# Moving a first-stage store from SyncE's DMA queue to ScalarE's, one butterfly into the next chunk

## The chip, the core and the metric

The kernel runs on one core of a Trainium2 chip. The metric is device microseconds of one execution, the median over runs. Within the core, PE (TensorE) does matmuls, DVE (VectorE), ACT (ScalarE) and POOL (GpSimd) do elementwise work, and SP (SyncE) only issues DMA transfers here. ACT can issue them too, in line with its own instructions. In the trace the transfers that SP issues are queue q1, and those of ACT queue q10; both are carried by the core's 16 DMA engines.

## The reference

```python
u = x * v                                   # x, v: [2, 12480, 128]
h = (np.maximum(pos_emb @ w1, 0) @ w2) * window   # the filter, [12480, 128]
y = np.fft.irfft(np.fft.rfft(u, n=2 * S, axis=1) * np.fft.rfft(h, n=2 * S, axis=0), n=2 * S, axis=1)[:, :S]
x = (x * y).reshape(24960, 128)
h = x @ w_in                                # [24960, 2048]
return np.maximum(0.01 * h, h) @ w_out      # [24960, 128]
```

A long convolution of two batches with one filter (through a Fourier transform), a product with x, and a two-layer MLP over all tokens, all in float32.

## The kernel before

The transform is split in two stages of sizes 98 and 128. **The first stage of batch 0**, the part that this change touches, transforms batch 0 and the filter together. It runs over 16 chunks `c` of `MC` = 4 columns. For a chunk,

- `load_a(c)` brings in the transform matrices `ft` and the tiles `xt` and `vt` (seven DMAs, three of them large: 300.1 KB, 384 KB and 384 KB; the others carry the few rows that don't fit the pattern). `load_pos` brings in the positions `pos` for four chunks at once (three DMAs, 768 KB the large one).
- `prep(c)` makes the operands two chunks ahead: on POOL the product `uh` = x·v and `q1`, on DVE `q2`, on both the second matrix `f1` from `q1` and `q2`, on PE `pt` and `hp` with ACT's copy `pts` between them, and on DVE the filter part of `uh`. It is a generator of which one piece follows each butterfly.
- four **butterflies** `mm` follow: eight matmuls into `a` (line 314), ACT's copy `a1s` (line 98), and DVE's sum and difference into the tile `o` (lines 100 and 102).
- `store` writes `o` to the scratch `scr1` in DRAM, two DMAs of 588 KB each (line 287).

The program is written out by hand (`manual_schedule`): on each engine the instructions stand in the order in which the code gives them, and each waits for what it needs. SP gives out loads and stores in one line: at the head of chunk `c` come `load_a(c + 3)`, the positions when due, in chunk 2 also six loads of constants (`mb`, `mi`, `mi2`), and only then the store of chunk `c - 1`, which was put off in the list `late`. The tile `o` has two buffers, so DVE can't begin chunk `c + 1` before the store of chunk `c - 1` has landed. `ft` has five, `xt` and `vt` three each. Every DMA raises one of eight counters (DMAHW0 to DMAHW7 in the rows below), which are dealt out in turn over both queues, and it waits until the DMA that had the same counter before it has landed; so at most eight are under way.

Behind the 16 chunks follow the second stage of batch 0 (it reads `scr1` into `bin`), and the first stage of batch 1 and the MLP, which are interleaved.

Of the kernel before, what the change touches and what calls it, by code (L numbers as in the profile page):

```python
# [20 lines left out]
MC = 4  # L21
# [6 lines left out]
def tile_conv_mlp(ctx, tc, x, v, pos_emb, w1, w2, w_in, w_out, cf, cr, cg, cb, ci, cw, out):  # L28
    nc = tc.nc
# [14 lines left out]
    scr1 = dram.tile([128, NA, 2 * C0], F32, name="scr1")  # L44
# [18 lines left out]
    def load_tokens(t, src, m0, n):  # L63

        full = src[: ROWS * NB, :].rearrange("(a p n) d -> a p n d", p=2, n=HB)
        for r in (slice(0, R0), slice(R0, ROWS)):
            nc.sync.dma_start(out=t[r], in_=full[r, :, m0:m0 + n, :])
        last = src[ROWS * NB + m0:ROWS * NB + m0 + n, :]
        nc.sync.dma_start(out=t[ROWS:], in_=last[None, None, :, :].to_broadcast([1, 2, n, last.shape[1]]))
# [24 lines left out]
    def add_sub(pool, a0, a1, dst0, dst1, view, bufs):  # L94

        a1s = pool.tile([128, 512], F32, tag="a1s", name="a1s", bufs=bufs)[:a1.shape[0]]
        n = a1.shape[1]
        nc.scalar.copy(a1s[:, :n], a1)  # L98
        yield
        nc.vector.tensor_tensor(out=dst0, in0=view(a0), in1=view(a1s[:, :n]), op=ALU.add)  # L100
        yield
        nc.vector.tensor_tensor(out=dst1, in0=view(a0), in1=view(a1s[:, :n]), op=ALU.subtract)

    def run(g):
        for _ in g:
            pass


    def chunk(c):
        k0 = c * KC  # L110
        return k0, min(KC, NA - k0)
# [46 lines left out]
    with tc.manual_schedule():  # L158
# [3 lines left out]
        def fetch_a(c):  # L162
            ft = s0.tile([128, MC1 * 4 * NA], F32, tag="s0", name="ft1", bufs=3)[:NA].rearrange(
                "a (m p e) -> a m p e", m=MC1, p=2)
            nc.sync.dma_start(out=ft, in_=cf[:, c * MC1:(c + 1) * MC1])
            xv = []
            for i, src in enumerate((x, v)):
                t = s0.tile([128, 1024], F32, tag=f"s{1 + i}", name="xv1", bufs=3 - i)[:NA, :2 * MC1 * D].rearrange(
                    "a (p m d) -> a p m d", p=2, d=D)
                load_tokens(t, src[1], c * MC1, MC1)  # L170
                xv.append(t)
            got[c] = ft, xv
# [3 lines left out]
        def mult_a(c):  # L176
            ft, (xt, vt) = got.pop(c)
            nc.gpsimd.tensor_tensor(out=xt, in0=xt, in1=vt, op=ALU.mult)
            u1[c] = ft, xt

        with ExitStack() as st:
# [5 lines left out]
            PQ = 16  # L187
# [3 lines left out]
            def load_pos(q):  # L191
                pos_t[q] = sba.tile([NA, 2, PQ, FO], F32, tag="pos", name="pos")
                load_tokens(pos_t[q], pos_emb, q * PQ, PQ)

            def load_a(c):
                ft = sba.tile([NA, MC, 2 * NA], F32, tag="ft", name="ft", bufs=5)
                nc.sync.dma_start(out=ft, in_=cf[:, c * MC:(c + 1) * MC, 0])
                xt = sba.tile([NA, 2, MC, D], F32, tag="xt", name="xt", bufs=3)
                vt = sba.tile([NA, 2, MC, D], F32, tag="vt", name="vt", bufs=3)
                load_tokens(xt, x[0], c * MC, MC)  # L200
                load_tokens(vt, v[0], c * MC, MC)
                f_t[c], xv_t[c] = ft, (xt, vt)
                if c < 2:
                    f1_t[c] = sba.tile([NA, MC, 2 * NA], F32, tag="f1", name="f1", bufs=3)
                    nc.sync.dma_start(out=f1_t[c], in_=cf[:, c * MC:(c + 1) * MC, 1])
# [41 lines left out]
            NC0 = HB // MC  # L247
# [12 lines left out]
            run(prep(1))  # L260
            late = []
            for c in range(NC0):
                if c + 3 < NC0:
                    load_a(c + 3)
                    if (c + 3) * MC % PQ == 0:
                        load_pos((c + 3) * MC // PQ)
                if c == 2:
                    nc.sync.dma_start(out=mb, in_=cb)
                    nc.sync.dma_start(out=mi, in_=ci)
                    for s in range(2):  # L270
                        for ri in range(2):
                            nc.sync.dma_start(out=mi2[HB * s:HB * s + HB, ri], in_=ci[HB * ri:HB * ri + HB, s])
                if c == 6:
                    for m, mh, ml in ((mb.rearrange("p s r q -> p s (r q)"), mb_h, mb_l), (mi, mi_h, mi_l)):
                        nc.scalar.copy(mh, m)
                        nc.vector.tensor_tensor(out=ml, in0=m, in1=mh, op=ALU.subtract)
                for f in late:
                    f()
                late = []
                uh, ft, f1 = uh_t.pop(c), f_t.pop(c), f1_t.pop(c)  # L280
                nxt = prep(c + 2) if c + 2 < NC0 else iter(())
                o = sba.tile([NA, 2, MC, 2, C0], F32, tag="o", name="o")

                def store(m0, n, o, c=c):
                    for ri in range(2):
                        r0 = HB * ri + c * MC + m0
                        nc.sync.dma_start(out=scr1[r0:r0 + n].rearrange("m k e -> k m e"),
                                          in_=o[:, ri, m0:m0 + n].rearrange("a m s d -> a m (s d)"))
                if c == 7:
                    w22 = s0.tile([128, D], F32, tag="mi", name="w22", bufs=1)  # L290
                    for i in range(2):
                        nc.sync.dma_start(out=w22[64 * i:64 * i + 64, :], in_=w2)
                if c == NC0 - 3:
                    fetch_a(0)

                    bin0 = s0.tile([128, MC1 * 4 * NA], F32, tag="s0", name="bin0", bufs=3)[
                        :, :KC * 2 * C0].rearrange("p (k s e) -> p k s e", k=KC, s=2)

                def early():
                    for ri in range(2):  # L300
                        rows = slice(HB * ri, HB * ri + HB - DIR * MC)
                        nc.sync.dma_start(out=bin0[rows], in_=scr1[rows, :KC, :].rearrange("p k (s e) -> p k s e", s=2))

                def direct(m, o, c=c):
                    for ri in range(2):
                        r0 = HB * ri + c * MC + m
                        nc.sync.dma_start(out=bin0[r0:r0 + 1], in_=o[:KC, ri, m])
                if c == NC0 - 1:
                    mult_a(0)
                for mm in range(MC):  # L310
                    a = psa.tile([NA, 2, 512], F32, tag="a", name="a", bufs=3)
                    for p, f, n in ((0, ft, NA), (1, f1, ROWS)):
                        for ri in range(2):
                            nc.tensor.matmul(a[:, p, C0 * ri:C0 * ri + C0], f[:n, mm, NA * ri:NA * ri + NA],  # L314
                                             uh[:n, p, mm], start=True, stop=True)
                    run(add_sub(sba, a[:, 0, :2 * C0], a[:, 1, :2 * C0], o[:, :, mm, 0, :], o[:, :, mm, 1, :],
                                lambda t: t.rearrange("a (r e) -> a r e", r=2), 2))
                    next(nxt, None)
                    if c >= NC0 - DIR:
                        direct(mm, o)  # L320
                    if c == NC0 - 1 and mm == EARLY:
                        early()
                    if c == NC0 - 1 and mm == MC - 1:
                        store(0, MC, o)
                if c < NC0 - 1:
                    late.append(lambda store=store, o=o: store(0, MC, o))
# [161 lines left out]
        with ExitStack() as st:  # L488
# [70 lines left out]
            late = []  # L559
# [40 lines left out]
            for c in range(NCH):  # L600
# [10 lines left out]
                late = []  # L611
                n = chunk(c)[1]
# [234 lines left out]
```

## Time and profile before

| | |
|---|---|
| median of 3 runs | 1793.81 us (1793.01 to 1794.57) |
| the profiled execution | 1797.53 us, of which its span is 1795.5 us |
| mean granted TensorE clock | 0.979 |
| PE busy over the span | 1714.1 us (95%) |
| DVE, ACT, POOL busy | 966.5, 892.5, 587.2 us (54%, 50%, 33%) |
| bytes moved by the DMA engines | 251.77 MB |

The table is of the whole span, most of which is the MLP, where PE is nearly always at work. The first stage of batch 0 takes about the first 167 us and is read by itself, in the rows below: times there are microseconds from the start of the span.

### The profile page before, as it was taken

The numbers are of one execution on the slowest core, as the hardware profiler recorded it, in microseconds if no ns is written. First come the engines' busy times: TensorE is split into PE (matmuls) and PEld (weight loads), VectorE is DVE, ScalarE is ACT, GpSimd is POOL, SyncE is SP. The second block draws the span as 40 slices with busy tenths as digits, with TensorE's granted clock in tenths as the row PEclk, the third lists the DMA queues.
The fourth block names the chain that finished last, engine by engine and source line by source line (L and its number), as shares of the span: only waits on it lengthen the run. The fifth ranks groups of instructions, "written<-read, shape, count | busy, mean of one in ns | idle before, by whom it ended". The sixth has DMA issues, their size and how long they took to land.

```text
span 1795.5 us, 29288 instructions
## 1 busy us (share of the span) xinstructions
PE 1714.1 (95%) x10620; PEld 1607.7 (90%) x10620; DVE 966.5 (54%) x1688; ACT 892.5 (50%) x1803; POOL 587.2 (33%) x450
## 2 busy tenths in 40 slices
PE   6787989879999999999999999999999999999998
PEld 6677545479999999999999999999999999999998
DVE  3566788845455555555555544444444444444444
ACT  1222444324445666666666666444444444444444
POOL 3453334213323555555544444211121111211120
PEclk8789999989999999999999999999999999999999
DMA  9898999786756465555555541212211122112210
GB/s 224 244 274 259 310 301 321 235 248 192 216 159 180 121 179 142 140 144 144 144 144 144 141 129 54 77 50 65 60 50 50 54 64 57 51 50 60 65 51 14
DMA packets 147707, 251.77 MB, mean 140 GB/s; under 512 B 10842, under 2 KB 96742, under 8 KB 144492
## 3 DMA queue, kind: packets, MB, share of 16 engines
q1 hardware_dynamic: 127420, 224.21, 44.8%
q10 hardware_dynamic: 20144, 25.69, 4.3%
q8 instruction: 84, 1.38, 0.3%
q14 instruction: 59, 0.48, 0.1%
HBM read 166.37 MB, written 83.43 MB: 139 GB/s over the span
## 4 chain that ended last, share of the span: by engine, by line
PE 84%; DMA 9%; DVE 3%; SPq 2%; issue 1%; ACT 1%; POOL 0%; ACTq 0%; POOLq 0%; DVEq 0%
PE mh L693 10%; PE mh L695 10%; PE mh L694 10%; PE acc L713 10%; PE acc L712 10%; PE acc L714 10%; PE yp L679 6%; PE cv L132 4%; PE cv L350 2%; DMA scr<-o 2%; PE up L117 2%; PE dp L139 2%; DMA xt<-in_x_dram 2%; PE op L723 2%; DMA ft<-in_cf_dram 1%; PE xp L671 1%
## 5 line engine op out<-in xcount | busy, mean ns | idle before, releaser
L699 DVE SCALAR_TENSOR_TENSOR rl<-mh,rh 128x390 fp32r<-128x390 f32 x1024 | 574.9, 564 | 616.6 <-ACT rh L698 614.9
L698 ACT ACTIVATE rh<-mh 128x390 fp32r<-128x390 f32 x1024 | 508.1, 498 | 387.3 <-PE mh L695 369.9
L693 PE MATMUL mh<-zh,w_in_h 128*128 128x390 f32 x1024 | 366.0, 357 | 0.0
L695 PE MATMUL mh<-zh,w_in_l 128*128 128x390 f32 x1024 | 350.2, 342 | 0.0
L694 PE MATMUL mh<-zl,w_in_h 128*128 128x390 f32 x1024 | 349.4, 341 | 0.0
L713 PE MATMUL acc<-rl,w_out_h 128*128 128x390 f32 x1024 | 348.8, 341 | 0.0
L712 PE MATMUL acc<-rh,w_out_h 128*128 128x390 f32 x1024 | 348.3, 340 | 0.0
L714 PE MATMUL acc<-rh,w_out_l 128*128 128x390 f32 x1024 | 348.2, 340 | 0.0
L686 POOL TENSOR_TENSOR zl<-zf,zh 128x390 fp32r<-128x390 f32 x63 | 64.9, 1030 | 706.1 <-ACT zh L685 706.1
L693 PEld LDWEIGHTS mh<-zh,w_in_h 128*128 128x128 f32 x1024 | 194.0, 189 | 2.2 <-DVE rl L699 0.2
L694 PEld LDWEIGHTS mh<-zl,w_in_h 128*128 128x128 f32 x1024 | 193.9, 189 | 2.2 <-DVE zl L686 0.2
L695 PEld LDWEIGHTS mh<-zh,w_in_l 128*128 128x128 f32 x1024 | 194.0, 189 | 0.0
L713 PEld LDWEIGHTS acc<-rl,w_out_h 128*128 128x128 f32 x1024 | 193.9, 189 | 0.0
L714 PEld LDWEIGHTS acc<-rh,w_out_l 128*128 128x128 f32 x1024 | 193.1, 189 | 0.0
L712 PEld LDWEIGHTS acc<-rh,w_out_h 128*128 128x128 f32 x1024 | 193.0, 188 | 0.0
L679 PEld LDWEIGHTS yp<-g,cp 98*128 98x128 f32 x1024 | 123.5, 192 | 0.0
L679 PE MATMUL yp<-g,cp 98*128 98x97 f32 (+1 forms) x1024 | 123.1, 274 | 0.0
L431 POOL TENSOR_TENSOR us<-us,hd 128x512 f32<-128x512 f32 (+1 forms) x50 | 63.6, 1272 | 146.2 <-ACT us L429 146.2
L685 ACT CAST zh<-zf 128x390 fp32r<-128x390 f32 x64 | 33.2, 519 | 148.8 <-DVE zf L684 148.8
L485 POOL TENSOR_TENSOR cp<-cin 98x512 f32<-98x512 f32 x63 | 88.4, 1402 | 0.0
L484 POOL TENSOR_TENSOR cp<-cin 98x512 f32<-98x512 f32 x63 | 81.5, 1293 | 17.5 <-DMA cin<-scr 9.4
L98 ACT COPY a1s<-a 98x384 f32<-98x384 f32 x64 | 30.6, 479 | 110.3 <-PE a L314 67.2
(129 smaller groups left out, 2149.9 us busy)
## 6 DMA issues: line engine op xcount, KB each, us to landing
cin<-scr SPq DMA_DIRECT2D x63, 392.0 KB
hd<-hspec SPq DMA_DIRECT2D x48, 512.0 KB
g<-in_cg_dram SPq DMA_DIRECT2D x64, 300.1 KB
scr<-o SPq DMA_DIRECT2D x32, 588.0 KB
bin<-scr SPq DMA_DIRECT2D x23, 768.0 KB
scr1b<-o SPq DMA_DIRECT2D x32, 392.0 KB
hspec<-hs ACTq DMA_DIRECT2D x48, 256.0 KB
scr<-ct ACTq DMA_DIRECT2D x24, 512.0 KB
```

Of the source, the lines that this page charges most:

```text
L132: nc.tensor.matmul(dst, u, w, start=(i == 0), stop=(i == 2))
L484: eng.tensor_tensor(out=o1, in0=c0, in1=c1, op=ALU.subtract)
L485: eng.tensor_tensor(out=o0, in0=c0, in1=c1, op=ALU.add)
L679: nc.tensor.matmul(yp[:, at:at + n], ci_t[:, r, m, p, :], g[:, r, p, m, :n], start=(r == 0), stop=(r == 1))
L693: nc.tensor.matmul(hp, w_in_h[:, fs], zh, start=True, stop=False)
L694: nc.tensor.matmul(hp, w_in_h[:, fs], zl, start=False, stop=False)
L695: nc.tensor.matmul(hp, w_in_l[:, fs], zh, start=False, stop=True)
L698: nc.scalar.activation(out=rh, in_=hp, func=AF.Relu)
L699: nc.vector.scalar_tensor_tensor(out=rl, in0=hp, scalar=0.0, in1=rh, op0=ALU.max, op1=ALU.subtract)
L712: nc.tensor.matmul(ap, w_out_h[:, f, :], rh, start=False, stop=False)
L713: nc.tensor.matmul(ap, w_out_h[:, f, :], rl, start=False, stop=False)
L714: nc.tensor.matmul(ap, w_out_l[:, f, :], rh, start=False, stop=(f == NF - 1))
```

## The change

The store goes from SP's queue to ACT's. It is given out inside the butterfly loop, behind the first butterfly (`mm` = 0) of the next chunk and ahead of that chunk's piece of `prep`; and the loads of chunk `c + 3`, with the positions, follow it there, where they stood at the chunk's head. The loads of constants in chunk 2 keep their place in the code, which is now ahead of that chunk's loads.

```diff
             for c in range(NC0):
-                if c + 3 < NC0:
-                    load_a(c + 3)
-                    if (c + 3) * MC % PQ == 0:
-                        load_pos((c + 3) * MC // PQ)
                 if c == 2:
...
-                for f in late:
-                    f()
-                late = []
...
-                        nc.sync.dma_start(out=scr1[r0:r0 + n].rearrange("m k e -> k m e"),
+                        nc.scalar.dma_start(out=scr1[r0:r0 + n].rearrange("m k e -> k m e"),
                                           in_=o[:, ri, m0:m0 + n].rearrange("a m s d -> a m (s d)"))
...
+                    if mm == 0:
+                        for f in late:
+                            f()
+                        late = []
+                        if c + 3 < NC0:
+                            load_a(c + 3)
+                            if (c + 3) * MC % PQ == 0:
+                                load_pos((c + 3) * MC // PQ)
                     next(nxt, None)
```

On ACT the difference begins in chunk 0: the first row of three copies is butterflies 2 and 3 of chunk 0 and butterfly 0 of chunk 1; `scr_60` is `scr1`, so that the rows with it are the stores of chunks 0 and 1 (minus: before, plus: after, with what each instruction waits for).

```order
 L98 COPY a1s<-a 98x384 [waits DVE_49,PE_49,Activation_49] x3
+L280 DMA scr_60<-o 98x4x384 [waits DMAHW3_49,DVE_49]
+L280 DMA scr_60<-o 98x4x384 [waits DMAHW5_49]
 L232 COPY pts<-pt 128x392 [waits PE_49]
-L98 COPY a1s<-a 98x384 [waits DVE_49,PE_49,Activation_49] x4
+L98 COPY a1s<-a 98x384 [waits PE_49,Activation_49]
+L98 COPY a1s<-a 98x384 [waits DVE_49,PE_49,Activation_49] x3
+L280 DMA scr_60<-o 98x4x384 [waits DMAHW5_49,DVE_49]
+L280 DMA scr_60<-o 98x4x384 [waits DMAHW0_49]
```

Two store instructions now stand on ACT between the copy of a chunk's first butterfly and its `pts`, and wait there for DVE's last difference of the chunk before (DVE_49) and for a counter each.

On SP, before, from the loads of chunk 5 on (they are given out in chunk 2), with the constants, the store of chunk 1 and the loads of chunk 6 behind them:

```order
L197 DMA ft<-in_cf_dram 98x4x196 [waits DMAHW1_49,PE_49]
L67 DMA xt<-in_x_dram 96x2x512 [waits DMAHW2_49,Pool_49]
L67 DMA xt<-in_x_dram 1x2x512 [waits DMAHW3_49]
L69 DMA xt<-in_x_dram 1x2x512 [waits DMAHW4_49]
L67 DMA vt<-in_v_dram 96x2x512 [waits DMAHW5_49]
L67 DMA vt<-in_v_dram 1x2x512 [waits DMAHW6_49]
L69 DMA vt<-in_v_dram 1x2x512 [waits DMAHW7_49]
L268 DMA mb<-in_cb_dram 128x256 [waits DMAHW0_49]
L269 DMA mi<-in_ci_dram 128x256 [waits DMAHW1_49]
L272 DMA mi_75<-in_ci_dram 64x128 [waits DMAHW2_49]
```

The same place after the change:

```order
L264 DMA mb<-in_cb_dram 128x256 [waits DMAHW3_49]
L265 DMA mi<-in_ci_dram 128x256 [waits DMAHW4_49]
L268 DMA mi_75<-in_ci_dram 64x128 [waits DMAHW5_49]
L268 DMA mi_75<-in_ci_dram 64x128 [waits DMAHW6_49]
L268 DMA mi_75<-in_ci_dram 64x128 [waits DMAHW7_49]
L268 DMA mi_75<-in_ci_dram 64x128 [waits DMAHW0_49]
L197 DMA ft<-in_cf_dram 98x4x196 [waits DMAHW1_49,PE_49]
L67 DMA xt<-in_x_dram 96x2x512 [waits DMAHW2_49,Pool_49]
L67 DMA xt<-in_x_dram 1x2x512 [waits DMAHW3_49]
L69 DMA xt<-in_x_dram 1x2x512 [waits DMAHW4_49]
L67 DMA vt<-in_v_dram 96x2x512 [waits DMAHW5_49]
L67 DMA vt<-in_v_dram 1x2x512 [waits DMAHW6_49]
```

The stores are gone from SP, and the constants stand ahead of the loads of chunk 5. The counters that the two `mi_75` rows with DMAHW5 and DMAHW0 wait for are those that the two stores of chunk 1 raise on ACT.

## Rows read from the trace of the kernel before

**Rows 1.** Busy time of each engine in stretches of the first stage: up to the start of chunk 3 on DVE, chunk 3, chunks 4 to 12, and chunks 13 to 15. The last columns are the granted clock, the mean busy share of the DMA engines and GB/s.

```profile
core 0: us, PE busy (x) PEld busy (x) DVE busy (x) ACT busy (x) POOL busy (x), PEclk, DMA share, GB/s
33.50:56.90 23.40, 17.52 (x109) 16.51 (x108) 13.03 (x23) 5.08 (x11) 12.33 (x8) 0.86 0.83 223
56.90:65.30 8.40, 7.22 (x31) 6.71 (x32) 5.82 (x12) 1.83 (x5) 4.29 (x3) 0.61 0.97 286
65.30:147.80 82.50, 69.55 (x412) 63.76 (x410) 53.10 (x102) 21.99 (x48) 44.93 (x28) 0.88 0.96 273
147.80:167.20 19.40, 15.57 (x82) 14.35 (x82) 13.60 (x27) 4.78 (x10) 3.61 (x3) 0.88 0.80 247
```

**Rows 2.** Who waited for whom on DVE from 35 to 168 us: total, times, longest.

```profile
DVE o L100 <- DMA scr<-o: 43.7, 12, 8.1
DVE o L100 <- ACT a1s L98: 4.4, 5, 1.7
```

**Rows 3.** DVE in order of time: start, duration, line. The last difference of chunk 1, the first sum of chunk 2, the last difference of chunk 2, then the first sum of chunks 3, 4, 6, 7, 13 and 15.

```profile
40.45 0.55 DVE L102 TENSOR_TENSOR o<-a,a1s 98x384 f32<-98x384 f32 x1
43.00 0.56 DVE L100 TENSOR_TENSOR o<-a,a1s 98x384 f32<-98x384 f32 x1 [2.01 <-DMA scr<-o]
48.27 0.54 DVE L102 TENSOR_TENSOR o<-a,a1s 98x384 f32<-98x384 f32 x1
56.91 0.56 DVE L100 TENSOR_TENSOR o<-a,a1s 98x384 f32<-98x384 f32 x1 [8.10 <-DMA scr<-o]
65.29 0.56 DVE L100 TENSOR_TENSOR o<-a,a1s 98x384 f32<-98x384 f32 x1 [2.57 <-DMA scr<-o]
86.60 0.56 DVE L100 TENSOR_TENSOR o<-a,a1s 98x384 f32<-98x384 f32 x1 [6.46 <-DMA scr<-o]
95.23 0.56 DVE L100 TENSOR_TENSOR o<-a,a1s 98x384 f32<-98x384 f32 x1 [2.82 <-DMA scr<-o]
147.79 0.56 DVE L100 TENSOR_TENSOR o<-a,a1s 98x384 f32<-98x384 f32 x1 [2.59 <-DMA scr<-o]
161.58 0.56 DVE L100 TENSOR_TENSOR o<-a,a1s 98x384 f32<-98x384 f32 x1 [3.39 <-DMA scr<-o]
```

**Rows 4.** The chain of work that ended last, where it runs over PE at its full clock in chunk 3 and 4 (16 matmuls are two butterflies), over the last store, and over the store of chunk 1: start, length.

```profile
50.19 6.60 DMA scr<-o
63.49 0.41 PE pt L229 x4
63.91 1.30 PE a L314 x8
65.21 0.88 PE hp L240 x8
169.25 5.64 DMA scr<-o
175.04 4.36 DMA bin<-scr
```

**Rows 5.** SP's queue in order of time: start, time to give out, line. The constants, the store of chunk 1 and the loads of chunk 6, then the positions and the store of chunk 4.

```profile
42.94 0.38 SPq L268 DMA_DIRECT2D mb<-in_cb_dram  x1
45.89 0.36 SPq L269 DMA_DIRECT2D mi<-in_ci_dram  x1
47.09 2.44 SPq L272 DMA_DIRECT2D mi<-in_ci_dram  x4
49.63 1.01 SPq L287 DMA_DIRECT2D scr<-o  x2
50.74 1.07 SPq L197 DMA_DIRECT2D ft<-in_cf_dram  x1
...
74.03 2.48 SPq L67 DMA_DIRECT2D pos<-in_pos_emb_dram  x2
77.42 0.57 SPq L69 DMA_DIRECT2D pos<-in_pos_emb_dram  x1
78.09 0.92 SPq L287 DMA_DIRECT2D scr<-o  x2
```

**Rows 6.** What the DMA engines moved in chunks 4 to 12 (65.3 to 147.8 us): the total, then by queue: packets, MB, share of 16 engines.

```profile
DMA packets 15259, 22.55 MB, mean 273 GB/s; under 512 B 799, under 2 KB 11411, under 8 KB 15252
q1 hardware_dynamic: 15252, 22.46, 95.8%
```

**Rows 7.** The same of a stretch of the second stage (274 to 282 us), in which SP's queue loads `xv` by the same pattern as `xt` and `vt` and ACT's queue stores.

```profile
DMA packets 1659, 3.14 MB, mean 392 GB/s; under 512 B 138, under 2 KB 650, under 8 KB 1658
q1 hardware_dynamic: 585, 1.60, 53.0%
q10 hardware_dynamic: 1073, 1.53, 52.0%
```

**Rows 8.** Columns as in rows 1, two short stretches of the first stage: one of loads of `vt` alone, one of stores alone.

```profile
104.00:106.00 2.00, 1.59 (x10) 1.30 (x9) 2.00 (x5) 0.58 (x2) 0.88 (x1) 1.00 0.99 235
158.00:160.00 2.00, 2.00 (x15) 2.00 (x14) 0.18 (x1) 0.91 (x2) 1.82 (x1) 1.00 0.91 330
```

**Rows 9.** DMA instructions by line: time to give one out, least, median and most, in ns. ACT's stores of the second stage, ACT's `hspec` stores there, and SP's stores of the first stage.

```profile
L148 ACTq DMA_DIRECT2D scr<-ct x22: 364/366/398, 191.1 to 337.3; - x22
L628 ACTq DMA_DIRECT2D hspec<-hs x50: 515/534/1242, 175.7 to 348.4; - x50
L287 SPq DMA_DIRECT2D scr<-o x32: 308/358/1010, 34.9 to 169.3; - x32
```

**Rows 10.** POOL's part of `prep` (chunks 4 to 12): count, busy, mean ns, idle time ahead of it and its releasers. Below it ACT's copy of the first butterfly of chunk 2, and PE's wait for the positions.

```profile
L212 POOL TENSOR_TENSOR uh<-xt,vt 98x1024 f32<-98x1024 f32 x9 | 21.7, 2410 | 19.2 <-DMA vt<-in_v_dram 8.2 <-DMA ft<-in_cf_dram 3.8 <-PE a L314 3.4
L221 POOL TENSOR_TENSOR q<-ft,rot 98x784 f32<-98x784 f32 x10 | 17.2, 1719 | 0.0
40.54 0.48 ACT L98 COPY a1s<-a 98x384 f32<-98x384 f32 x1 [0.82 <-PE a L314]
82.91 0.89 PE L229 MATMUL pt<-ident,pos 98*128 98x98 f32 x4 [3.71 <-DMA pos<-in_pos_emb_dram]
```

## The prediction

> **What bounds the kernel now.** I read the stretches of the first stage first, then DVE's waits, DVE's order of time, SP's queue, and last the DMA queues. In chunks 4 to 12 the DMA engines are busy 0.96 of the time, while DVE works 53.1 of 82.5 us, ACT 22.0 and PE 69.6, a part of that at half clock (granted 0.88 in the mean) [rows 1]. So the stage runs at the pace of its transfers. The place where that is felt is DVE: it waits 12 times, 43.7 us in all, for a store to land before it may write `o` again, and only 4.4 us for ACT [rows 2].
>
> Without waits a chunk takes less than the 9.17 us it has on average between the starts of chunks 4 and 13 ((147.79 - 65.29)/9) [rows 3]. On PE it is four butterflies of 1.30 us, `pt` with 0.41 and `hp` with 0.88, together 6.5 us at full clock [rows 4]; on DVE 53.1/9 = 5.9 us [rows 1].
>
> Two things make a store late. SP gives it out late: the pair of chunk 1 is ready at 41.0 us (DVE's last difference ends at 40.45 + 0.55) [rows 3] and goes out at 49.63, behind the loads of chunk 5 and six loads of constants; the pair of chunk 4 goes out at 78.09, behind the positions [rows 5]. Then it stands in one queue behind those loads. The DMA engines themselves do 2.51 MB per chunk (22.55/9) at 273 GB/s [rows 6].
>
> **The change part by part.** *Issue on ACT.* 30 of the 32 store instructions move into ACT's line ahead of `pts` and the next copy; the last pair moves to ACT too, at the end. ACT gives out a transfer in 0.37 us at the shortest form and about 0.53 at the `hspec` form (SP needs 0.36 for these stores) [rows 9], so about 0.9 us per chunk with the gap between two. ACT works 22.0/82.5 of the time, 2.4 us per chunk [rows 1]; DVE meanwhile has a butterfly (two of about 0.5 us) and `q2`. I cost it at nothing; if that cover were gone it would be 0.9 us for each of 15 chunks, 13.5 us. No store stood in ACT's line in this stage before, so that is the bound of this term.
>
> *The rate of the transfers.* Before, every transfer of this stage is in q1. Loads of `vt` alone run at 235 GB/s and stores alone at 330, both with the engines nearly full (0.99 and 0.91) [rows 8]. With loads of that same pattern in q1 and stores in q10 at once, the second stage moves 392 GB/s, halves of it in either queue [rows 7]. These are the bounds of the new rate: 273, as now, and 392, which would do a chunk's 2.51 MB in 6.4 us. The store rows and the loads here have other row lengths than there, so I take neither end, but about 320, 7.9 us per chunk; that is nearer to the old row, because the loads also have to wait for free counters.
>
> Here a rule of the Trainium skill stands against the change. "DMA: Bandwidth & Descriptors", section "Issuing engines are not separate DMA queues", says that transfers of ACT, SP and POOL run on the same 16 engines, and that giving them out on several "will only save the time on the sequencer it takes to initiate the DMA". By it the rate would stay at 273 GB/s, which is rival 1 below. The 392 GB/s of rows 7 speak against it, without settling it, as the transfers there are not the same.
>
> *How soon a store lands.* Free of SP it goes out 0.3 us after DVE's last difference. Alone it needs 7.2 us from there (given out at 49.63, chunk 3 starts on it at 56.91 [rows 3, 5]; its transfer is 6.60 us on the chain [rows 4], the last store's 5.64). With loads beside it longer; I take 9. As `o` has two buffers, two chunks take 0.3 + 9 + one chunk's own 6.5 us: 15.8, or 7.9 us per chunk, which happens to be the 320 GB/s above. With 7.2 it is 7.0.
>
> *Chunks 2 and 3.* The constants now stand ahead of the loads of chunk 5, and two of them wait for counters that the stores of chunk 1 raise. ACT can send that pair when the copy of butterfly 0 of chunk 2 is done (41.0 us) [rows 10] and the store of chunk 0 has landed, which let DVE start at 43.0 [rows 3]; say 43, landed at 43 + 7.2 = 50.2. DVE could begin chunk 3 there instead of at 56.9. But the fourth `mi` load and the loads of chunk 5 go out only then; they take about 4 us to give out and 2 to land: 56.2. POOL's product and `q1` follow (2.41 + 1.72 [rows 10]): 60.3, and DVE, which waits for `q1` in the middle of chunk 3, still has about 3 us to do: chunk 4 starts at 63.4 instead of 65.3, a gain of 1.9 us. If the store of chunk 0 lands 1.6 us earlier on its own queue, which the shorter line ahead of it allows, it is 3.5. I take 3. So most of the 8.1 us of rows 3 is given back to the late loads.
>
> *Chunks 4 to 12.* Nine chunks of 7.9 instead of 9.17 us: 9 x 1.27 = 11.4 us less. From this goes the wait for the positions: in chunk 6 PE waits for them until 82.9 us [rows 10]. They now wait for a counter of the store of chunk 4, go out some 5 us earlier than at 74.03 [rows 5], and the chunk still stops for them; the stop costs PE its clock as it does now (0.61 in the stretch behind the long wait of chunk 3 [rows 1]). I charge 4.5 us. Left: 6.9 us.
>
> *Chunks 13 to 15 and the end.* There 7.9 us per chunk would be no better than the 19.4 us of now for three [rows 1]; the 3.39 us wait ahead of chunk 15 [rows 3] may go, and the last store, whose landing after 5.64 us releases the second stage [rows 4], stays last. I put 0, with 0 to 3 us of gain.
>
> Sum: 3 + 6.9 + 0 = 9.9 us, about 10. Nothing behind it depends on absolute time: the second stage and the MLP begin when the last store has landed and move forward as a whole. Against the profiled execution, 1797.5 us, this gives 1787.5; that execution stands 3.7 us above the median of the runs, so against the median 1793.8 it is **1784 us**.
>
> **The rivals.** *1. The transfers stay at their rate.* Then only the stretches can gain in which the engines are not full: 0.83 until chunk 3 and 0.80 from chunk 13 on, against 0.96 between [rows 1]. That is 23.4 x 0.13/0.96 = 3.2 us and 19.4 x 0.16/0.96 = 3.2; the first goes back to the late loads of chunk 5. About 3 us remain: 1791. For it speak the 0.96 and the skill's rule; against it rows 7.
>
> *2. Slower: the loads now wait for the stores.* The counters are shared, and after the change a load often has to wait for a store of the chunk just finished, with POOL's 4.1 us still to come after it. If a store beside loads lands later than 11.5 us after it was given out, two chunks take 0.3 + 11.5 + 6.5 = 18.3 us, as now; that is the point from which it decides. At 13.5 us a chunk takes 10.2, and nine of them 9 us more, to which the 3 us of chunks 2 and 3 are no longer gained: about 1802. For it speaks that POOL already waits 8.2 us for `vt` in this stretch [rows 10]; against it that a store needs only 7.2 alone.
>
> *3. The full rate.* At 392 GB/s the transfers need 6.4 us per chunk, and with stores that land in 7.2 a chunk takes 7.0: 9 x 2.2 = 19.5 us, and with 3 + 2 for the ends about 22 us: 1772.
>
> **How the numbers follow.** Runs of this kernel lie within 0.1% of their median; 0.2%, 3.6 us, is about what can be told from no change. Chances: the forecast (1777 to 1789) 0.58, rival 1 0.18, rival 2 0.14, rival 3 0.10. The forecast and rival 3 are faster by more than 0.2%; of rival 1 a fifth is, the rest is within 0.2%, and so is a little of rival 2. Faster 0.71, same 0.17, slower 0.12. The range that leaves out 2 in 10 goes from 1773 (into rival 3) to 1797 (past rival 1, into the nearer part of rival 2); the forecast's own is 1777 to 1789.
>
> **What would show it.** Right: the stores under ACT's queue, with q10 carrying near half of the bytes of chunks 4 to 12; over 300 GB/s there; DVE's waits for stores well under 43.7 us; a new wait in chunk 3 of DVE's second matrix for POOL's `q1`, which started late; chunk 4 near 63, chunk 13 near 138, the start of the second stage's `bin` loads near 165. Wrong: a rate near 273 GB/s (rival 1); waits of ACT's copies or of POOL's product for loads that add up to more than DVE's store waits lose (rival 2). If ACT is held by a full queue when it gives out the second of a pair, the 0.9 us per chunk becomes several, and that alone could turn the sign.

## The result, and the profile after

The changed kernel takes 1805.8 us (median; 1803.0 to 1808.9) against 1794.2 (1793.0 to 1796.7) of the kernel before: 1.0063 times as long, 95% interval 1.0044 to 1.0083. It is slower by 11.6 us, where 1784 was forecast. The profiled execution took 1805.71 us, its span is 1803.6 (1795.5 before).

The same stretches as in [rows 1], cut at the same chunk starts on DVE (chunks 1 to 2, chunk 3, chunks 4 to 12, and from chunk 13 to the last store; columns as there):

```profile
32.90:56.06 23.16, 17.88 (x88) 16.55 (x88) 14.24 (x23) 4.81 (x10) 8.94 (x6) 0.75 0.74 215
56.06:65.24 9.18, 7.93 (x51) 7.11 (x49) 5.88 (x11) 2.31 (x5) 5.34 (x3) 1.00 0.86 266
65.24:154.58 89.34, 68.88 (x396) 64.21 (x396) 59.43 (x101) 21.56 (x47) 51.17 (x27) 0.89 0.86 258
154.58:173.90 19.32, 16.73 (x104) 15.30 (x104) 15.91 (x27) 5.67 (x12) 8.45 (x4) 1.00 0.75 241
```

Chunk 4 starts where it started before (65.24 against 65.29). Chunks 4 to 12 take 89.34 us instead of 82.5, and the DMA engines are busy 0.86 of that instead of 0.96. That is 6.8 of the 8.1 us by which the span grew; the rest falls behind chunk 13.

Who waited for whom from 35 to 174 us, on DVE (against [rows 2]), POOL, PE, and on SP's queue:

```profile
DVE o L100 <- ACT a1s L98: 25.2, 13, 5.7
DVE f L236 <- POOL q L221: 14.7, 8, 3.8
DVE o L100 <- DMA scr<-o: 4.8, 4, 1.7
...
POOL uh L212 <- DMA vt<-in_v_dram: 23.4, 5, 10.7
...
PE pt L229 <- DMA pos<-in_pos_emb_dram: 13.5, 3, 5.2
PE hp L240 <- ACT pts L232: 11.1, 9, 3.1
...
SPq L67 <- DMA scr<-o: 17.8, 6, 6.2
SPq L268 <- DMA scr<-o: 6.3, 1, 6.3
SPq L197 <- DMA scr<-o: 5.2, 2, 3.6
SPq L69 <- DMA scr<-o: 2.2, 2, 1.9
```

DVE's wait for stores has all but gone, as forecast: 4.8 us instead of 43.7. In its place DVE waits 25.2 us for ACT's copies and 14.7 for POOL's `q1`, POOL waits for `vt` (23.4), and SP's queue stands 31.5 us (the last four rows) with a load in hand until a store has landed. Such a load needs a counter that a store of ACT's queue still holds.

DVE also works longer: 59.43 us in chunks 4 to 12 instead of 53.10. Most of that is `q2`, the product that DVE makes for the second matrix (from 35 to 170 us, before and after):

```profile
L221 DVE TENSOR_TENSOR q<-ft,rot 98x784 f32<-98x784 f32 x13 | 14.0, 1075 | 0.0
L221 DVE TENSOR_TENSOR q<-ft,rot 98x784 f32<-98x784 f32 x13 | 22.9, 1763 | 0.0
```

In both traces `q2` takes 0.97 us where POOL is idle as it starts. Where POOL's product or `q1` is already at work, `q2` ends 0.8 to 0.9 us after POOL does (in the changed kernel one `q2` runs from 100.92 to 103.11, and POOL's `q1` ends at 102.28). POOL's work, now later, lengthens `q2` 8 times in 13 instead of twice.

Stations of the chain of work that ended last, and SP's queue around chunk 4 (start, length or time to give out):

```profile
41.72 6.63 DMA scr<-o
48.37 0.53 SPq L268
...
65.65 10.39 DMA scr<-o
76.11 0.61 SPq L67
...
83.63 6.06 DMA pos<-in_pos_emb_dram
89.83 0.89 PE pt L229 x4
```

```profile
72.62 0.35 SPq L197 DMA_DIRECT2D ft<-in_cf_dram  x1
76.11 1.27 SPq L67 DMA_DIRECT2D xt<-in_x_dram  x2
...
82.36 1.23 SPq L67 DMA_DIRECT2D pos<-in_pos_emb_dram  x2
```

Store, load, store, load: the store of chunk 3 takes 10.39 us, the `xt` loads go out only then, 3.1 us after the transfer ahead of them had been given out, the positions behind them, and PE gets its positions at 89.83, 6.9 us later than in [rows 10].

What the engines moved in chunks 4 to 12 (against [rows 6]):

```profile
DMA packets 15541, 23.05 MB, mean 258 GB/s; under 512 B 819, under 2 KB 11516, under 8 KB 15534
## 3 DMA queue, kind: packets, MB, share of 16 engines
q1 hardware_dynamic: 8226, 12.13, 47.3%
q10 hardware_dynamic: 7308, 10.84, 38.3%
```

Near half of the bytes are in q10, as forecast, but the rate has fallen from 273 to 258 GB/s. For a full engine it is 258/0.86 = 300, against 273/0.96 = 284.

### The profile page after: what moved, and what is told of

Read it like the earlier page. It is cut to its first block, busy times and chain, and to the rows that moved or that the text cites. A ratio compares the mean times of both kernels' runs of the same rounds, so it can differ in the third digit from the quotient of the medians.

```text
span 1803.6 us, 29292 instructions
## 1 busy us (share of the span) xinstructions
PE 1717.2 (95%) x10620; PEld 1611.5 (89%) x10620; DVE 981.1 (54%) x1688; ACT 893.6 (50%) x1803; POOL 596.7 (33%) x450
## 4 chain that ended last, share of the span: by engine, by line
PE 84%; DMA 7%; DVE 4%; SPq 2%; issue 1%; ACT 1%; POOL 0%; ACTq 0%; POOLq 0%
PE mh L694 10%; PE mh L696 10%; PE mh L695 10%; PE acc L714 10%; PE acc L713 10%; PE acc L715 10%; PE yp L680 6%; PE cv L132 4%; PE cv L351 3%; PE up L117 2%; DMA scr<-o 2%; DMA vt<-in_v_dram 2%; PE op L724 2%; DMA xt<-in_x_dram 2%; PE dp L139 1%; PE xp L672 1%
## 5 line engine op out<-in xcount | busy, mean ns | idle before, releaser
L485 POOL TENSOR_TENSOR cp<-cin 98x512 f32<-98x512 f32 x63 | 81.5, 1293 | 16.7 <-DMA cin<-scr 16.6
L446 POOL TENSOR_TENSOR pl<-p,ph 128x512 fp32r<-128x512 f32 (+1 forms) x50 | 62.8, 1274 | 40.3 <-ACT ph L445 40.1
```

The lines of the kernel that those rows point to most:

```text
L485: eng.tensor_tensor(out=o1, in0=c0, in1=c1, op=ALU.subtract)
```

## The experiments

Ratios are to the kernel before, timed on the same chip; brackets are 95% intervals. In kernels that move the 4-KB transfers, line numbers are one or two higher (L101 is L100 here).

**Parts of the change.** *e1: loads at the head of the chunk again, ahead of the constants.*

```diff
@@ for c in range(NC0):
+                if c + 3 < NC0: load_a(c + 3); ...load_pos
@@ if mm == 0:
-                        if c + 3 < NC0: load_a(c + 3); ...load_pos
```

> Edit: the changed kernel with the loads of the chunk three ahead given out at the head of the chunk again, ahead of the constants; the stores stay on ACT behind butterfly 0. Theory (loads are held on SP's queue by the completion counters of the stores, which SP's and ACT's transfers share): the loads of chunks 6 and later keep the counters that they have in the changed kernel, so the long holds in chunks 4 to 12 stay; only the constants no longer stand ahead of the loads of chunk 5. About 1803 us, between 1799 and 1806. Rival A (ACT loses the time: the stores stand ahead of its copies): as the changed kernel, 1806. Rival C (giving the loads out a butterfly later is what costs): back to 1794 or faster.

Measured: 1810.7 us, 1.0079 [1.0055, 1.0103], above the range given and within the noise of the changed kernel. With the stores off SP's queue, where the loads stand in the program hardly matters. Chunk 4 now starts at 63.49 on DVE, 1.8 us sooner, and chunk 13 again at 154.6: a lead won early is lost in the middle.

*e2: order alone.*

```diff
-                        nc.scalar.dma_start(out=scr1[r0:r0 + n]...
+                        nc.sync.dma_start(out=scr1[r0:r0 + n]...
```

> Edit: the changed kernel with the stores on SP's queue; the order in the program is that of the changed kernel (store behind the next butterfly 0, loads behind the store). Theory (counters): the last load of chunk c+4 has to wait for the first store of chunk c, as in the changed kernel, one chunk earlier than before the change; the DMA engines starve, and one queue has no faster mix: 1803 to 1812 us, DMA share of chunks 4 to 12 below 0.92. Rival A (ACT's line is what costs): no store stands in ACT's line, so 1790 to 1796. Rival B (the mix of two queues is slower than one): 1794 or faster.

Measured: 1820.7 us, 1.0142 [1.0125, 1.0160], slower than any bound given. In one queue the loads stand behind a store that waits for DVE's last difference (27.6 us in all); the engines are busy 0.83 in chunks 4 to 12, at 232 GB/s:

```profile
68.60:168.20 99.60, 70.13 (x394) 66.92 (x393) 57.83 (x102) 21.56 (x47) 47.27 (x27) 0.81 0.83 232
```

*e3: queue alone* (the kernel before, and only this line):

```diff
-                        nc.sync.dma_start(out=scr1[r0:r0 + n]...
+                        nc.scalar.dma_start(out=scr1[r0:r0 + n]...
```

> Edit: the kernel before with its stores on ACT's queue; they stand at the head of the chunk as before, behind the loads in the program. Theory (counters): the loads wait for the same stores' counters as in the changed kernel, so SP's queue is held 20 to 30 us by stores in the stage and the time is that of the changed kernel within 5 us: 1802 to 1811; the difference to it is what ACT loses when it stands behind DVE's last difference at the head of each chunk. Rival A (ACT's line): clearly slower than the changed kernel, 1812 or more, since ACT now waits for the end of DVE's chunk ahead of the first copy. Rival C (the later place of the loads is what costs): 1784 to 1792.

Measured: 1812.9 us, 1.0097 [1.0077, 1.0118]: the queue alone makes it slower, and neither part by itself gains. The time lies just inside what rival A asked for: ACT's copies wait 35.7 us for stores here (35 to 168 us), 0.8 us in the changed kernel. Together the two parts cost less than either alone. A likely reading, which these waits support and no run tried apart, is that the place behind butterfly 0 spares ACT that wait, and the queue of their own spares the loads the wait for the store to go out (e2).

*p1: q1 ahead of the product on POOL* (the changed kernel):

```diff
@@ def prep(c):
-                (nc.gpsimd if c else nc.vector).tensor_tensor(out=uh[:, :, :, FO:], in0=xt, in1=vt, op=ALU.mult)
@@ behind q1, q2
+                (nc.gpsimd if c else nc.vector).tensor_tensor(out=uh[:, :, :, FO:], in0=xt, in1=vt, op=ALU.mult)
```

> Edit: the changed kernel with the product x * v (L212) behind q1 (L221) on POOL; q1 needs only the first-stage matrices and the rotation, the product needs the loads that come last in a chunk. Theory (counters): the loads are as late as in the changed kernel, but DVE's sum f (L236) no longer waits for q1 behind the product (14.7 us in the changed kernel between 33 and 175 us); the product itself is needed only two chunks on. Some 6 to 13 us less than the changed kernel: 1793 to 1800. Rival A (ACT's line): the wait for q1 was only where ACT's lateness showed; within 3 us of the changed kernel.

Measured: 1808.2 us, 1.0075 [1.0053, 1.0096]: no gain, where 6 to 13 us were expected. DVE's wait for `q1` (14.7 us) is gone from the trace, and PE waits for the positions 28.1 us instead of 13.5. The wait moved.

**Loads without the stores' counters.** *g1: stores on POOL,* whose transfers count on counters of their own:

```diff
-                        nc.scalar.dma_start(out=scr1[r0:r0 + n]...
+                        nc.gpsimd.dma_start(out=scr1[r0:r0 + n]...
```

> Edit: the changed kernel with the stores given out by POOL instead of ACT, at the same place in the program. In the program POOL's transfers count on completion counters of their own, so no load waits for a store. Theory (shared counters hold the loads): SP's queue waits 0 us for the landing of a store in the stage (31 us in the changed kernel), the DMA share of chunks 4 to 12 is back at 0.93 or more; if a store on POOL costs no more than one on ACT, 1780 to 1792 us. What POOL needs to give a transfer out is not known: at more than 2 us per store it would become the bound, with 1800 or more, and SP's waits would tell that apart from the rivals. Rival C (loads and stores of the same chunk get in each other's way at the DMA engines, counters or not): the DMA share stays near 0.86 and the time near 1806.

Measured: 1809.9 us, 1.0082 [1.0065, 1.0100]. SP waits for no store any more, and it is no faster: POOL now stands at the store with the product and `q1` behind it, and DVE's `q2` comes behind them 8 times in 13, 3.3 to 5.5 us each (42.6 us in all, against 14.0 before).

```profile
POOL scr L280 <- DVE o L102: 39.0, 14, 3.5
L221 DVE TENSOR_TENSOR q<-ft,rot 98x784 f32<-98x784 f32 x13 | 42.6, 3273 | 0.0
```

*g2: the four 4-KB transfers of a chunk on POOL,* so that five transfers per chunk share the eight counters, *and g3: the same on the kernel before.*

```diff
@@ load_tokens, for xt and vt of batch 0
-            nc.sync.dma_start(out=t[r], in_=full[r, :, m0:m0 + n, :])
+            (nc.sync if r.start == 0 else nc.gpsimd).dma_start(out=t[r], in_=full[r, :, m0:m0 + n, :])
-        nc.sync.dma_start(out=t[ROWS:], in_=last...
+        nc.gpsimd.dma_start(out=t[ROWS:], in_=last...
```

> Edit: the changed kernel with the four 4-KB transfers of a chunk (rows 96 and 97 of xt and vt) given out by POOL; SP gives out three loads per chunk and ACT two stores. With five transfers per chunk on the eight shared counters instead of nine, the first load that waits for a store waits for one three or more chunks back. Theory (shared counters): SP waits under 5 us for stores, chunks 4 to 12 have a DMA share of 0.93 or more, 1780 to 1792 us, unless four transfers per chunk cost POOL more than about 4 us. Rival A (ACT's line) and rival C (contention at the engines): 1800 or more.

> Edit: the same on the kernel before (the four 4-KB transfers of a chunk given out by POOL), as the control for the run with that edit on the changed kernel: it holds what the edit itself costs on POOL and saves on SP. Theory (shared counters): in the kernel before the loads hardly wait for stores' counters (2.6 us), so there is little to gain but SP's own time: 1788 to 1797. The difference of the two is then the gain of the change without the held loads: the changed kernel with the edit 5 to 12 us ahead of this one. Rivals A and C: this one 8 us or more ahead.

Measured: g2 1803.8 us, 1.0050 [1.0032, 1.0067]; g3 1789.6 us, 0.9971 [0.9960, 0.9981]. The edit helps the kernel before; on the changed one its gain is within the noise, against the theory. In g2 SP's queue still stands 19.6 us for stores (31.5 in the changed kernel, under 5 expected). The loads are nearly in time all the same (POOL's wait for `vt` is 5.3 us instead of 23.4), but DVE waits for stores again and PE for `pts`:

```profile
DVE o L101 <- DMA scr<-o: 22.0, 7, 5.9
...
PE hp L241 <- ACT pts L233: 24.3, 11, 6.6
```

So late loads are one cost and not the whole.

*t1: pts ahead of the stores on ACT* (the changed kernel; the three lines `for f in late` stand behind `next(nxt, None)`):

```diff
@@ if mm == 0:
-                        for f in late: f()
-                        late = []
                         if c + 3 < NC0: load_a(c + 3) ...
                     next(nxt, None)
+                    if mm == 0:
+                        for f in late: f()
+                        late = []
```

> Edit: the changed kernel with the copy of pts ahead of the stores in ACT's line instead of behind them. Rival A (ACT's line): PE's wait for pts ahead of hp (11 us on PE, 9 times) goes, and 5 to 11 us with it: 1795 to 1801. Theory (shared counters): that wait lay beside late loads anyway; what changes the time is which counters the loads get, and here the stores of chunks 1 to 4 wait for each other's counters while loads wait for stores only at chunks 4, 6, 8 and 10: chunk 5 starts up to 4 us earlier than in the changed kernel, and the end is within 5 us of it: 1800 to 1808.

Measured: 1812.4 us, 1.0092 [1.0074, 1.0111]. PE's wait for `pts` is gone, and nothing is won: ACT's copies now wait 10.5 us behind the stores, and PE for the positions 22.4 us. Not the gain that ACT's line as the sole cause would give.

**Two costs taken away, and the third buffer.** *h1: g2 and t1 together; h2: g1 and t1 together* (on POOL that puts the store behind the product and `q1`).

> Edit: the changed kernel with the 4-KB transfers on POOL (which alone gave 1803.8 us, with SP's waits for stores down, but with PE waiting 24.3 us for pts, which stands behind the stores on ACT), and the copy of pts put ahead of the stores. Theory K (ACT's line is the second cost: a store waits there for the counter of an earlier store or for DVE's last difference, and pts, hp and the next butterflies stand behind it): PE's wait for hp goes, 1786 to 1794 us, level with the control of the kernel before (1789.6). Theory N (a store that shares the engines with loads that run ahead lands late, 9.4 to 13.4 us, wherever it stands): DVE's waits for stores stay over 20 us and the time is 1798 to 1806.

> Edit: the changed kernel with the stores on POOL, behind the product and q1 of chunk c+2 instead of ahead of them (ahead, POOL waited 41 us for DVE's last difference with that work behind it: 1809.9 us). No counter is shared with the loads and ACT gives out nothing. Theory K (a store in an in-order line costs what stands behind it): POOL's wait at the store falls under 10 us, PE's wait for POOL's f (18.6 us) goes: 1785 to 1796 us. Theory N (contention at the engines): DVE then waits for stores, which land 10 us or more after they are given out, and the time stays at 1800 or more.

Measured: h1 1800.2 us, 1.0026 [1.0016, 1.0037]; h2 1797.7 us, 1.0010 [0.9992, 1.0027], with runs from 1788 to 1803. From g1 to h2, 0.7% goes with what stands behind the store in POOL's line (`q2` falls from 42.6 to 16.7 us with it, in the fastest of the ten runs, which is the one profiled). In h1 the waits for stores are 27.0 us on DVE, and on its chain of waits a store beside loads takes 12 to 13 us:

```profile
65.69 12.53 DMA scr<-o
...
94.15 13.08 DMA scr<-o
```

In the kernel before, the stores on that chain take 5.40 to 7.55 us (two of them in [rows 4]), with the younger loads behind them in the same queue.

*o3: three buffers of `o`,* on the changed kernel and on the one before.

```diff
-                o = sba.tile([NA, 2, MC, 2, C0], F32, tag="o", name="o")
+                o = sba.tile([NA, 2, MC, 2, C0], F32, tag="o", name="o", bufs=3)
@@ load_a: xt and vt
-                ... bufs=3)
+                ... bufs=2)
```

> Edit: the changed kernel with three buffers of o instead of two (xt and vt get two instead of three for the room). Held loads (the counters) as the cause: DVE waits only 4.8 us for stores in the changed kernel, so there is nothing for a third buffer to give; the loads keep their counters: 1800 to 1808 us. Theory N (late landing of the stores sets the pace of chunks 4 to 12): the landing has a chunk more to hide in, 1790 us or faster.

> Edit: the same on the kernel before, as the control: DVE's 43.7 us of waits for stores should nearly go. If those waits were what the kernel lost (as the prediction took it), 1775 to 1785 us. If the transfers were full anyway (DMA share 0.96 in chunks 4 to 12), the wait turns up at POOL's product or PE's positions and only the stretches with free engines give something: 1788 to 1795.

Measured: changed 1808.9 us, 1.0072 [1.0050, 1.0093]; before 1794.4 us, 0.9994 [0.9983, 1.0004]. The second is the run that decides on the forecast. All waits of DVE in it from 35 to 168 us:

```profile
DVE o L100 <- ACT a1s L98: 21.7, 13, 7.7
DVE f L236 <- POOL q L221: 10.5, 8, 5.8
DVE q L221 <- DMA ft<-in_cf_dram: 0.7, 1, 0.7
```

The 43.7 us of waits for stores are gone, with the stores still on SP, and the kernel is as fast as before. What the engines move between the starts of chunks 4 and 13 is the same too, 272 GB/s at 0.95 busy against 273 at 0.96:

```profile
55.80:143.70 87.90, 66.76 (x398) 63.85 (x397) 60.64 (x103) 21.53 (x47) 50.46 (x27) 0.84 0.95 272
```

In place of the waits for stores DVE has those for ACT and `q1` above, and a longer `q2` (25.8 us instead of 14.0). So the waits were where a stage that was full of transfers let its slack be seen. The edit also takes a buffer each from `xt` and `vt`; what that costs by itself was not run, and the unchanged rate is what speaks against a gain hidden by it.

**What is left.** *k1: h1 with xt and vt in two buffers instead of three. k2: k1 and three buffers of `o`. k3: g3 with the o3 edit. k4: h2 with the o3 edit.*

> Edit: the kernel with the 4-KB transfers on POOL and pts ahead of the stores on ACT (1800.2 us), with two buffers of xt and vt instead of three, so that SP's loads can run one chunk less ahead. Theory N (the stores land late, 12 to 13 us on the chain of waits of that kernel, because loads that are not needed yet share the engines with them): DVE's waits for stores fall well below 27.0 us and the time to 1792 to 1798. If running ahead is not what costs: the loads are later and nothing else changes, 1800 to 1808.

> Edit: as the run before it, and three buffers of o. Now no load waits long for a store's counter, PE does not wait for pts, and a store has a chunk more to land in. What is left is the rate at which two queues move the bytes. If the mix is faster by as much as the prediction took (320 against 273 GB/s): 1780 us or faster, 8 us or more ahead of the control with the same edits on one queue. If the mix gives only what the busy share shows (about 307 against 298 GB/s for a full engine in the two kernels without the third buffer): within 4 us of the control.

> Edit: the kernel before with the 4-KB transfers on POOL (1789.6 us), and three buffers of o, two of xt and vt: the control of the run before it, with the stores on SP's queue. The third buffer gave nothing on the kernel before (1794.4), since the transfers filled the engines 0.95 of the time; the same is expected here: 1787 to 1791 us.

> Edit: the kernel with the stores on POOL behind q1 (1797.7 us, 1788 to 1803), and three buffers of o, two of xt and vt. No counter is shared, ACT gives nothing out. Theory N (late landing beside loads that run ahead): DVE's waits for stores (29.6 us) go and the time falls to 1782 to 1792. If the rate is the limit: 1793 to 1800, as with two buffers.

Measured: k1 1797.0 us, 1.0010 [0.9998, 1.0021]; k2 1794.5, 0.9987 [0.9977, 0.9997]; k3 1788.5, 0.9958 [0.9943, 0.9972]; k4 1789.6, 0.9969 [0.9953, 0.9985]. Chunks 4 to 12 of the four, in that order:

```profile
64.30:145.30 81.00, 67.32 (x413) 63.10 (x411) 65.77 (x101) 21.90 (x48) 65.05 (x61) 0.94 0.95 290
```

```profile
61.60:142.60 81.00, 68.58 (x401) 64.81 (x401) 72.06 (x102) 21.13 (x47) 66.52 (x62) 0.88 0.94 290
```

```profile
58.40:137.20 78.80, 65.17 (x397) 62.23 (x396) 73.17 (x103) 21.61 (x47) 62.80 (x61) 0.89 0.96 291
```

```profile
57.80:135.50 77.70, 65.13 (x398) 61.99 (x397) 64.58 (x103) 21.53 (x47) 62.33 (x46) 0.89 1.00 298
```

This is the rate nearly by itself. Two queues with ACT's stores move 290 GB/s at 0.95 and 0.94 busy, one queue (k3) 291 at 0.96: for full engines 305 and 309 against 303. The second queue moves no more bytes in the time, and some 2% more for the time that the engines are busy. In k3 DVE is busy 73.17 of 78.80 us (`q2` alone takes 34.5 us in the first stage), so that there the transfers may not be the only limit. Letting the loads run less far ahead (k1) took DVE's waits for stores from 27.0 to 17.2 us and the time from 1.0026 to 1.0010; the intervals overlap, so that share is likely rather than shown.

*k5 and k6: the positions loaded one chunk earlier,* in k3 and k4.

```diff
-                    if (c + 3) * MC % PQ == 0:
-                        load_pos((c + 3) * MC // PQ)
+                if (c + 4) * MC % PQ == 0 and c + 4 < NC0:
+                    load_pos((c + 4) * MC // PQ)
```

> Edit: the control with stores on SP, the 4-KB transfers on POOL and three buffers of o (1788.5 us), with each block of positions loaded one chunk earlier. In it PE still waits 6.9 us for positions, and the stop costs it clock. If the engines' bytes alone set the pace (0.96 busy between the starts of chunks 4 and 13), the wait turns up at the next load and the time stays at 1786 to 1790. If the stop at the positions costs by itself (the prediction put 4.5 us on it): 1782 to 1786.

> Edit: the same on the kernel with the stores on POOL behind q1 and three buffers of o (1789.6 us), where PE waits 10.3 us for positions. Bytes as the limit (1.00 busy at 298 GB/s there): 1786 to 1791. The stop as a cost by itself: 1779 to 1785.

Measured: k5 1785.4 us, 0.9955 [0.9943, 0.9967] (k3 was 0.9958); k6 1790.6 us, 0.9980 [0.9966, 0.9993] (k4 was 0.9969). PE's waits for the positions are gone in both (6.9 and 10.3 us), and nothing is won: the 1785.4 us lie in the range for a cost of its own, but the kernel before was faster on that chip too (1794.4 against 1797.0), so the ratio decides. The stop at the positions is no cost of its own in a full stage. k5 has the lowest ratio of all, level with k3 and 0.45% ahead of the kernel before, with the stores on SP's queue.

**The pairs side by side**, stores on ACT against stores on SP with the same edits otherwise (three `o` means two buffers of `xt` and `vt` as well):

| edits | on ACT | on SP |
|---|---|---|
| none | 1.0063 | 1 |
| three `o` | 1.0072 | 0.9994 |
| 4-KB transfers on POOL | 1.0050 | 0.9971 |
| the same, `pts` ahead of the stores | 1.0026 | (no stores there; 0.9971) |
| the same, three `o` (`pts` ahead of the stores on ACT) | 0.9987 | 0.9958 |

In every pair ACT is the slower, by 0.3 to 0.8%. Stores on POOL behind `q1`, which share no counter with the loads and do not stand in ACT's line, are not slower than on SP: 1.0010 against 1 with two buffers of `o` (h2), and 0.9969 against 0.9994 with three (k4 and o3_before, whose intervals just touch). So the loss is not that of a second queue as such. Likely it goes with the shared counters and ACT's line; POOL's stores also went in fewer packets, and which share is whose was not tried apart.

## Why the prediction was wrong

**What bounds the kernel: the bytes right, the place wrong.** The first paragraph said that the stage runs at the pace of its transfers (0.96 busy), and the third then built the time from DVE's waits for stores. These two do not go together. o3_before shows it: the 43.7 us vanish and the time stays. The recurrence "0.3 + 9 + 6.5 us for two chunks" described the waits and not the pace.

**The rate: the step that failed.** It put 320 GB/s between 273 and 392, 7.9 us for a chunk in chunks 4 to 12; measured were 258 GB/s and 9.9 us (89.34/9). The rows of [rows 8] gave the answer if weighed by bytes: of the 2.51 MB of a chunk 1.20 are stores (two of 588 KB, 330/0.91 = 363 GB/s for full engines) and 1.31 loads (235/0.99 = 237), so 3.3 + 5.5 = 8.8 us, or 284 GB/s, which is just what one queue did before (273/0.96). So the engines were nearly full, and a second queue could gain only what it does to the rate of full engines. After the change that was 300, with most holds gone 305 and 309 (k1, k2), and on one queue with the same edits 303 (k3): little to win. The 392 of [rows 7] came from another mix: SP gave out one `xv` load (384 KB) there beside `bin` (768 KB) and two weight tiles (256 KB each), and 39% of the packets are under 2 KB (650 of 1659), in [rows 6] 75%. Their size alone does not explain the rate, since packets of 2 KB in q1 took 84 ns in the mean there, 138 in chunks 4 to 12 before the change and 107 after it; why was not tried. Rival 1 had the rate nearly right, but not the time, which it put at 1791. The Trainium skill ("DMA: Bandwidth & Descriptors", "Issuing engines are not separate DMA queues") says that transfers given out by several engines run on the same 16 engines and interleave; 290 GB/s on two queues against 291 on one agrees.

**Chunks 4 to 12: +6.8 instead of -6.9 us.** At 0.96 busy the stretch would have taken 89.34 x 0.86/0.96 = 80.0 us; the 9.3 us are engines without work, more than the 6.8 us by which the stretch grew. Three costs came with the queue, each seen in a trace: loads held by the stores' counters (31.5 us on SP), what stands behind a store in an in-order line (PE's 11.1 us for `pts`; 39.0 us on POOL in g1), and stores that share the engines with younger loads (10.39 us on the chain, up to 13.08 in h1). Taking one away alone brought nothing that can be told (g2, t1, o3_after); g2 and t1 together, fewer loads ahead and a third `o` brought 1.0063 to 0.9987. A part of that is worth as much on SP: k3, with the same edits there, is at 0.9958. So ACT's loss fell from 0.63 to 0.29%, by about half. That taking one cost away shows nothing and taking all away does, speaks for costs that take turns, each hidden behind the others. The last 0.3% stay open: in k2 ACT's copies still wait 12.9 us behind stores, and SP's queue 9.3 us in `xt` and `vt` loads; neither was tried apart.

**How soon a store lands: about right.** 9 us were taken; on the chain it is 4.26 to 10.39 us up to chunk 13, and DVE's wait fell to 4.8 us. The point from which rival 2 was to decide (11.5 us) was not reached on the chain, and it came out slower anyway: that price left out that the chunk's own stretch grows. It was taken as 6.5 us; chunk 3 took 9.2 (56.06 to 65.24) with almost no wait for a store, 3.1 of it for POOL's `q1`.

**Issue on ACT: size right, price wrong.** A pair takes 0.82 us there, 0.9 was said. The price of nothing left out how long the store itself waits in ACT's line.

**Chunks 2 and 3: 0 instead of -3 us.** The store of chunk 1 landed at 48.35, sooner than the 50.2 forecast, and chunk 4 started at 65.24. The late loads that were charged are those of chunk 5, and they came (POOL waited 10.7 us for their `vt`); but the last loads of chunk 4 were held as well, by the store of chunk 0, and the positions stood behind them, so that PE, and with it DVE, stopped in the middle of chunk 2 already:

```profile
37.27 1.23 SPq L67 DMA_DIRECT2D vt<-in_v_dram  x2
...
39.15 1.23 SPq L67 DMA_DIRECT2D pos<-in_pos_emb_dram  x2
```

```profile
46.34 0.89 PE L229 MATMUL pt<-ident,pos 98*128 98x98 f32 x4 [5.19 <-DMA pos<-in_pos_emb_dram]
```

e1 got 1.8 us back there and lost them by chunk 13.

**Positions: the stop was seen rightly** (PE at 89.83), **the 4.5 us were not its price**: k5 and k6 take the load forward and gain nothing. **Chunks 13 to 15**: 0 was said; from the start of chunk 13 to the loads of `bin` that follow the last store it takes about 1.4 us longer than before (28.7 against 27.3).

**Rival 2** had the sign and the first of the three costs, at a chance of 0.14; the time lies beyond the range, which ended at 1797.

## What to carry to other kernels

Where the transfer engines are nearly always busy (0.96 here), a wait for a transfer on a compute engine may be slack and not cost; here 43.7 us of it could be taken away for nothing. So price such a change in bytes over the rate of full engines, weighed by kind, before anything else. A queue of its own for stores moved hardly more bytes here, and it gave up the order by need that one queue has: loads that nobody needed yet went beside a store that somebody waited for, the counters tied the two together, and the engine that gave out a store had its own line held behind it. Fewer transfers on the busy queue helped (g3) where ACT's queue did not.

## What the runs showed that was not expected

Moving four transfers of 4 KB per chunk from SP's queue to POOL, 0.15 of the 22.05 MB of chunks 4 to 12, made the kernel before 0.29% faster (g3) and raised the rate of a full engine from 284 to 298 GB/s (283/0.95); why was not tried. Stores given out by POOL went in fewer packets (3161 for 10.85 MB in k4, 7308 for 10.84 in the changed kernel) and at three buffers of `o` the kernel is the faster by 0.25% for them (k4 against o3_before); whether by the packets or by what else differs there (the counters, the order in SP's queue) is open. And ten runs of h2 spread over 0.8%, about twice as far as those of the kernel before on the same chip; the cause stays open.
